# A Fourier mixing layer and a gated expert on one core: the last step's products and buffers, one bank's copy and the first seeds put in another order

## The chip, the cores and the metric

The kernel runs on one core of a Trainium2 chip. A core has five engines with queues of their own: TensorE (PE for its matmuls, PEld for its weight loads, which overlap them), VectorE (DVE), ScalarE (ACT), GpSimd (POOL) and SyncE (SP), which here issues nearly all DMAs. The metric is the device time of one execution in microseconds: the median of the timed runs. Where the profile is quoted, times are microseconds from the start of its span.

## The reference

```
def _attn_ref(x):                      # x: (8, 3008, 256)
    X = np.fft.fft(x, axis=1)
    X = np.fft.fft(X, axis=2)
    return X.real.astype(np.float32)

def _moe_ref(x, w_in, w_out):          # x: (24064, 256), w_in: (256, 2048), w_out: (2048, 256)
    h = x @ w_in
    g = h * np.cos(h)
    return (g @ w_out).astype(np.float32)
```

The output of the first function, reshaped to (24064, 256), is the input of the second. All values are float32.

## The kernel before

For each of the 8 batches, `transform` computes a real two-stage Fourier transform along the sequence (`fold`, `first_half`, a trip through DRAM, `second_half`), and the transform along the 256 columns is folded into the first weight matrix (`WC` for the cosine part, `WS` for the sine part). The work of the next batch's transform is spread over the steps of the current batch.

**Groups, steps, units.** A batch has 6 groups of up to 256 sequence positions: T = 225 columns in group 0, 256 in the others. A group has 8 steps (fp = 0 to 7), each for 256 of the 2048 hidden features, in two halves (u = 0, 1) of 128. There are 8 x 6 x 8 = 384 steps and 768 halves. The main loop (lines 763 to 829) runs over k; one pass is called a unit here. In unit k several halves are at work, in different stages:

- the current half k: two products on TensorE into a PSUM bank H, `mm1(cur, 0)` with WC (L466) and `mm1(cur, 1)` with WS, the first on top of a seed, that ACT wrote there before (`seed`, L447); ACT doubles the first (`act_e`, L478), and DVE makes the mirrored side (`dve_h`, L482);
- half k-1: ACT rounds (`act_round`, L494), DVE takes the fraction (`dve_frac`, L498), ACT takes the sine (`act_sin`, L504);
- half k-2: DVE multiplies (`dve_g`, L508), and after a step's second half POOL forms sums of the results (`sums`, L524 to L531; on DVE for the very last step);
- the step that is LAG = 5 units back: `mm2` (L557), seven output products m = 0 to 6, which accumulate over a group's 8 steps in four PSUM banks M (m = 0, 1; 2, 3; 4, 5; 6). With d, v = divmod(k - 5, 2), a unit with v = 0 runs m = 0 to 2 and, after `mm1(cur, 1)`, m = 3; a unit with v = 1 runs m = 4 to 6.

Every matmul in float32 is two passes; 256 columns take 0.216 us a pass, 225 take 0.190.

**The end of a group.** When a group's last step has gone through `mm2`, its four banks are copied to SBUF by `take_m`: in the unit with v = 1, bank 0 by ACT (L580) and bank 1 by DVE (L582); in the next unit, bank 2 by ACT and bank 3 (one product) by DVE. In the order before, the DVE copies are the last thing that a unit records, behind L498 and L482. POOL then combines the seven products to four outputs (`combine_m`, L597 to L612), and `store_out` transposes them on DVE (L654) into a buffer `ob` (two of them) and stores them with 16 DMAs on SP (L664). There are eight PSUM banks, four tagged M and four tagged H, and the next group takes the four M banks over as they are released.

**The very end.** The last group is combined by `combine_last` on DVE (L622 to L629), some of it straight from PSUM, transposed on TensorE (L639), copied from PSUM by ACT and DVE to the same two buffers `ob` (L642, L643), and stored with eight DMAs (L646), six on SP and two on ACT.

**The start.** For the first units the seeds need no matmul result, but they wait behind other work on ACT. In units 2 to 4 the first product of the next half, `mm1(nxt, 0)`, and its `act_e` are recorded ahead of the current half's `mm1(cur, 1)`, and behind the previous half's sine.

An engine's instructions run in the order in which the kernel records them; semaphores between engines are placed by the framework.

Of the kernel before, what the change touches and what calls it, by code (L numbers as in the profile page):

```python
# [11 lines left out]
FP = mybir.dt.float32  # L12
AF = mybir.ActivationFunctionType
ALU = mybir.AluOpType

BIG = 12582912.0
TWO_PI = 2.0 * math.pi
# [11 lines left out]
AHEAD = LAG + 1  # L29
# [64 lines left out]
def _runs(g, sg):  # L94


    runs = []
    for j, n, c in _cols(g):
        a, k = c, 0
        if sg:  # L100
            a, j = 256 - c - n, (N2 - j) % N2
            if j == 0:
                a, k, n = a + 1, 33, 31
        runs.append((a // 32, j, k, n))
    return runs
# [3 lines left out]
def kernel(  # L109
# [7 lines left out]
    nc = tc.nc  # L117
# [84 lines left out]
    def psum(name, tag="H"):  # L202
        return ppool.tile([128, 512], FP, tag=tag, bufs=bank[tag], name=name)
# [271 lines left out]
    def act_e(h):  # L475
        T = h.s.T
        h.ew = spool.tile([128, 256], FP, tag="ew", bufs=2, name="ew")
        nc.scalar.mul(out=h.ew[:, 0:T], in_=h.H[:, 0:T], mul=2.0)  # L478
# [17 lines left out]
    def dve_frac(h):  # L496
        r, y = sides(h)
        nc.vector.scalar_tensor_tensor(  # L498
            out=r, in0=r, scalar=-BIG, in1=y, op0=ALU.add, op1=ALU.subtract
        )  # L500

    def act_sin(h):
        r, _ = sides(h)
        nc.scalar.activation(out=r, in_=r, func=AF.Sin, bias=0.0, scale=SIN_SCALE)  # L504
# [13 lines left out]
    def sums(s):  # L518
        T = s.T
        s.S = spool.tile([128, 1024], FP, tag="S", bufs=3, name="S")  # L520
        gv, sv = blocks(s)
        qv = s.r[:, 0 : 4 * T].rearrange("p (q t) -> p q t", q=4)
        tt = (nc.vector if s is steps[-1] else nc.gpsimd).tensor_tensor
        tt(  # L524
            out=sv[:, 0:2],
            in0=qv[:, 1:2].to_broadcast([128, 2, T]),
            in1=qv[:, 0:4:3],
            op=ALU.subtract,
        )
        tt(out=sv[:, 2], in0=sv[:, 1], in1=gv[:, 0, 0], op=ALU.subtract)  # L530
        tt(out=sv[:, 3], in0=gv[:, 1, 0], in1=sv[:, 2], op=ALU.add)  # L531

    acc = {}
    started = {}

    def mm2(s, lo, hi):
        T = s.T
        key = (s.b, s.grp)
        if s.fp == 0 and lo == 0:
            acc[key] = []  # L540
            started[key] = set()
        gv, sv = blocks(s)
        todo = (
            (0, wv[:, 0, 0, s.fp], gv[:, 0, 0]),
            (1, wv[:, 1, 0, s.fp], gv[:, 1, 0]),
            (2, vx[:, 3, s.fp], gv[:, 1, 1]),
            (3, vx[:, 1, s.fp], sv[:, 0]),
            (4, vx[:, 0, s.fp], sv[:, 1]),
            (5, vx[:, 2, s.fp], sv[:, 2]),
            (6, wv[:, 1, 1, s.fp], sv[:, 3]),  # L550
        )
        for m, w, a in todo[lo:hi]:
            first = m // 2 not in started[key]
            if first:
                acc[key].append(psum("M", "M"))
            started[key].add(m // 2)
            nc.tensor.matmul(  # L557
                acc[key][m // 2][:, 256 * (m % 2) : 256 * (m % 2) + T],
                lhsT=w,
                rhs=a,  # L560
                start=first,
                stop=s.fp == 7,
                skip_group_check=True,
            )

    outs = {}
# [3 lines left out]
    def take_m(s, k, eng):  # L570
        T = s.T
        key = (s.b, s.grp)
        if k == 0:
            mrs[key] = spool.tile([128, 7 * 256], FP, tag="mr", bufs=1, name="mr")
        mv = mrs[key].rearrange("p (m t) -> p m t", m=7)[:, :, 0:T]
        m = 1 if k == 3 else 2
        to = mv[:, 2 * k : 2 * k + m]
        at = acc[key][k].rearrange("p (m t) -> p m t", m=2)[:, 0:m, 0:T]
        if eng is nc.scalar:
            eng.mul(out=to, in_=at, mul=TWO_PI)  # L580
        else:
            eng.tensor_scalar(out=to, in0=at, scalar1=TWO_PI, scalar2=None, op0=ALU.mult)  # L582
# [30 lines left out]

    def combine_last(s):
        key = (s.b, s.grp)
        M5, M3 = acc[key][2], acc[key][3]
        mv = mrs.pop(key).rearrange("p (m t) -> p m t", m=7)
        outs[key] = spool.tile([128, 7 * 256], FP, tag="cb", bufs=1, name="cb")
        cv = outs[key].rearrange("p (m t) -> p m t", m=7)
        tt, stt = nc.vector.tensor_tensor, nc.vector.scalar_tensor_tensor  # L620
        more = dict(op0=ALU.mult, op1=ALU.add)
        tt(out=cv[:, 0], in0=mv[:, 0], in1=mv[:, 1], op=ALU.add)  # L622
        stt(out=cv[:, 4], in0=M5[:, 256:512], scalar=-TWO_PI, in1=mv[:, 0], **more)
        stt(out=cv[:, 6], in0=M5[:, 0:256], scalar=TWO_PI, in1=cv[:, 4], **more)
        stt(out=cv[:, 1], in0=M3[:, 0:256], scalar=TWO_PI, in1=cv[:, 6], **more)
        store_last(s, 0)
        tt(out=cv[:, 5], in0=cv[:, 4], in1=mv[:, 3], op=ALU.add)
        tt(out=cv[:, 2], in0=cv[:, 5], in1=mv[:, 2], op=ALU.add)
        stt(out=cv[:, 3], in0=M5[:, 0:256], scalar=TWO_PI, in1=cv[:, 5], **more)  # L629
        store_last(s, 1)  # L630

    def store_last(s, sg):
        cv = outs[s.b, s.grp].rearrange("p (m t) -> p m t", m=7)
        ob = spool.tile([128, 512], FP, tag="ob", bufs=2, name="ob")
        ov = ob.rearrange("t (h c j) -> t h j c", h=2, j=2)
        pos = [psum("po", "H").rearrange("t (z j c) -> t z j c", z=2, j=2)[:, 0] for _ in "ab"]
        for j in range(2):
            for h in range(2):
                nc.tensor.transpose(  # L639
                    pos[h][:, j], cv[:, 2 * sg + j, 128 * h : 128 * h + 128], ident  # L640
                )
        nc.scalar.copy(out=ov[:, 0], in_=pos[0])  # L642
        (nc.vector.tensor_copy if sg else nc.scalar.copy)(out=ov[:, 1], in_=pos[1])  # L643
        for t0, j, k, m in sorted(_runs(s.grp, sg)):
            h, r0 = divmod(32 * t0, 128)
            (nc.scalar if sg and h else nc.sync).dma_start(  # L646
                out=out_r[s.b, j, k : k + m, :],
                in_=ob[r0 : r0 + m, 256 * h : 256 * h + 256],
            )
# [113 lines left out]
    for k in range(2 * n + LAG):  # L763
        t, u = divmod(k, 2)
        d, v = divmod(k - LAG, 2)
        cur, prev, old, nxt = unit(k), unit(k - 1), unit(k - 2), unit(k + 1)
        done = step(d)
        full = step(d if v else d - 1, True)
        if cur:
            if k % (2 * per) == 0:  # L770
                todo = transform(cur.s.b + 1) if cur.s.b + 1 < NB else {}
            if k not in range(3, AHEAD):
                mm1(cur, 0)
                if t == 0:
                    seed_first(cur)
                act_e(cur)
            if k == 0:
                spread_nb()
                fold_weights(1, 3)
            elif k == 1:  # L780
                pw = weights(0, 3)
            elif k == 2:
                pw = weight_row(3)
        if done:
            mm2(done, 4 * v, 4 * v + 3)
        if old:
            dve_g(old)
            if old.u:
                sums(old.s)
        if nxt and 0 < k < AHEAD - 1:  # L790
            seed(nxt)
        if prev:
            act_round(prev)
        if nxt and k >= AHEAD - 1:
            seed(nxt)
        if full:
            take_m(full, 0 if v else 2, nc.scalar)
        if prev:
            dve_frac(prev)
            act_sin(prev)  # L800
        if k == 1:
            keep_weights(0, 3, pw)
        elif k == 2:
            keep_wn(3, pw)
        if k + 1 in range(3, AHEAD):
            mm1(nxt, 0)
            act_e(nxt)
        if cur:
            mm1(cur, 1)
        if done and v == 0:  # L810
            mm2(done, 3, 4)
        if cur:
            dve_h(cur)
        if full:
            take_m(full, 1 if v else 3, nc.vector)
        if u == 0:
            continue
        for i in range(6):
            s = step(t - 4 - i, True)
            if s:  # L820
                combine_m(s, i)
        for sg, lag in ((0, 8), (1, 10)):
            s = step(t - lag, True)
            if s:
                store_out(s, sg)
        for call in opening.pop(t, ()):
            call[0](*call[1:])
        for call in todo.pop(t % per, ()):
            call[0](*call[1:])
# [31 lines left out]
```

## Time and profile before

| what | value |
|---|---|
| median of 3 runs | 1972.82 us (1972.72 to 1973.25) |
| the profiled execution | 1971.85 us |
| its span, first to last instruction | 1970.1 us |
| instructions | 29746 |
| busy: DVE, ACT, POOL | 1465.1, 1495.8, 1395.7 us |
| granted TensorE clock, mean | 0.997 |
| DMA traffic | 88.71 MB, 45 GB/s on the mean |

The four groups of TensorE instructions with the most busy time, by the page (line, engine, operation, output<-inputs, shapes, count | busy, mean ns of one | idle before):

```profile
L557 PE MATMUL M<-S,VX 128*128 128x256 f32 (+1 forms) x2304 | 612.3, 375 | 0.0
...
L466 PE MATMUL H<-pq,WC 128*128 128x256 f32 (+1 forms) x1536 | 458.4, 380 | 1.8 <-ACT H L447 1.8
L466 PE MATMUL H<-pq,WS 128*128 128x256 f32 (+1 forms) x1536 | 451.0, 375 | 0.0
...
L557 PE MATMUL M<-r,w 128*128 128x256 f32 (+1 forms) x1536 | 388.7, 375 | 0.0
```

A matmul's length here is 0.375 us, while the next one starts after 0.216: they are pipelined, so their ends overlap, and idle time before them is nearly nothing. The span is 1.75 us shorter than the time of the execution that it belongs to.

### The profile page before, as it was taken

What the parts mean: (1) busy time and instruction counts of PE and PEld (TensorE: products, weight loads), DVE (VectorE), ACT (ScalarE), POOL (GpSimd) and SP (SyncE); (2) the same over time, 40 slices, a digit from 0 to 9 for tenths busy, and PEclk for the clock granted to TensorE, in tenths of its full rate; (3) what the DMA queues carried; (4) which work ended last, traced back from release to release, by engine and by line L of the source; (5) the groups of instructions that cost most, each with busy time, mean ns of one, the idle gap of its engine ahead of it and who ended that gap; (6) DMA issues with size and microseconds to landing.
All of it is one profiled execution on the core that took longest, in us unless ns stands there. A gap on an engine that the chain in (4) does not pass through costs nothing.

```text
span 1970.1 us, 29746 instructions
## 1 busy us (share of the span) xinstructions
PE 1956.8 (99%) x9360; PEld 1684.9 (86%) x9360; DVE 1465.1 (74%) x2524; ACT 1495.8 (76%) x3360; POOL 1395.7 (71%) x1593
## 2 busy tenths in 40 slices
PE   9999999999999999999999999999999999999998
PEld 4988889888988889888898888988889888898887
DVE  3777778777777777777777777777777777788786
ACT  3777778777777777777777777777777777777775
POOL 3777767777677866787668776687767777666675
PEclk9999999999999999999999999999999999999999
DMA  8412022121211321112221221113111231100001
GB/s 198 97 41 57 21 51 48 38 51 35 51 38 34 57 40 44 35 36 56 42 41 35 51 49 36 38 40 66 29 39 37 56 58 24 38 22 15 11 16 29
DMA packets 176690, 88.71 MB, mean 45 GB/s; under 512 B 103303, under 2 KB 173622, under 8 KB 174902
## 3 DMA queue, kind: packets, MB, share of 16 engines
q1 hardware_dynamic: 176374, 86.68, 21.2%
q8 instruction: 76, 1.25, 0.3%
q14 instruction: 80, 0.66, 0.1%
q10 hardware_dynamic: 160, 0.13, 0.0%
HBM read 49.50 MB, written 37.27 MB: 44 GB/s over the span
## 4 chain that ended last, share of the span: by engine, by line
PE 97%; DMA 1%; SPq 1%; ACT 0%; DVE 0%; issue 0%; POOL 0%; DVEq 0%; POOLq 0%
PE M L557 58%; PE H L466 34%; PE pz L243 3%; PE pb L296 2%; DMA xp<-in_x_dram 1%; SPq L664 0%; PE pw L357 0%; DMA wr<-in_moe_w_in_dram 0%; PE pd L413 0%; DVE r L498 0%; DMA out_dram<-ob 0%; ACT r L504 0%; ACT r L494 0%; ACT H L447 0%; DVE xf L219 0%
## 5 line engine op out<-in xcount | busy, mean ns | idle before, releaser
L524 POOL TENSOR_TENSOR S<-r 128x512 f32<-128x512 f32 (+1 forms) x383 | 474.7, 1239 | 468.3 <-DVE r L508 429.1
L498 DVE SCALAR_TENSOR_TENSOR r<-r,H 128x512 f32<-128x512 f32 (+1 forms) x768 | 519.2, 676 | 287.9 <-ACT r L494 260.4
L504 ACT ACTIVATE r<-r 128x512 f32<-128x512 f32 (+1 forms) x768 | 477.9, 622 | 260.9 <-DVE r L498 258.6
L557 PE MATMUL M<-S,VX 128*128 128x256 f32 (+1 forms) x2304 | 612.3, 375 | 0.0
L508 DVE SCALAR_TENSOR_TENSOR r<-H,r 128x512 f32<-128x512 f32 (+1 forms) x768 | 517.9, 674 | 90.7 <-ACT r L504 39.2
L557 PEld LDWEIGHTS M<-S,VX 128*128 128x128 f32 x2304 | 437.7, 190 | 50.0
L466 PE MATMUL H<-pq,WC 128*128 128x256 f32 (+1 forms) x1536 | 458.4, 380 | 1.8 <-ACT H L447 1.8
L466 PE MATMUL H<-pq,WS 128*128 128x256 f32 (+1 forms) x1536 | 451.0, 375 | 0.0
L494 ACT ACTIVATE r<-H 128x512 f32<-128x512 f32 (+1 forms) x768 | 448.4, 584 | 0.4 <-DVE H L482 0.3
L482 DVE TENSOR_TENSOR H<-ew,H 128x256 f32<-128x256 f32 (+1 forms) x768 | 325.4, 424 | 100.2 <-PE H L466 20.1
L557 PE MATMUL M<-r,w 128*128 128x256 f32 (+1 forms) x1536 | 388.7, 375 | 0.0
L447 ACT ACTIVATE H<-nb,wn 128x256 f32<-128x256 f32 (+1 forms) x766 | 366.7, 479 | 0.0
L478 ACT ACTIVATE ew<-H 128x256 f32<-128x256 f32 (+1 forms) x768 | 288.9, 376 | 82.7 <-PE H L466 76.1
L466 PEld LDWEIGHTS H<-pq,WC 128*128 128x128 f32 x1536 | 278.6, 190 | 80.8 <-issue 42.8
L557 PEld LDWEIGHTS M<-r,w 128*128 128x128 f32 x1536 | 298.8, 197 | 29.7 <-ACT mr L580 1.3
L466 PEld LDWEIGHTS H<-pq,WS 128*128 128x128 f32 x1536 | 292.2, 190 | 32.3 <-issue 0.7
L530 POOL TENSOR_TENSOR S<-S,r 128x256 f32<-128x256 f32 (+1 forms) x383 | 275.3, 719 | 30.0
L531 POOL TENSOR_TENSOR S<-r,S 128x256 f32<-128x256 f32 (+1 forms) x383 | 274.4, 716 | 30.0
L557 PE MATMUL M<-r,VX 128*128 128x256 f32 (+1 forms) x768 | 228.7, 379 | 0.2
L557 PE MATMUL M<-S,w 128*128 128x256 f32 (+1 forms) x768 | 225.2, 375 | 0.0
L557 PEld LDWEIGHTS M<-r,VX 128*128 128x128 f32 x768 | 142.2, 190 | 25.4 <-issue 10.1
L557 PEld LDWEIGHTS M<-S,w 128*128 128x128 f32 x768 | 150.5, 196 | 14.6
(67 smaller groups left out, 918.0 us busy)
## 6 DMA issues: line engine op xcount, KB each, us to landing
out_dram<-ob SPq DMA_DIRECT2D x728, 32.0 KB
xp<-in_x_dram SPq DMA_DIRECT2D x56, 256.0 KB
zd<-zs SPq DMA_DIRECT2D x112, 96.0 KB
z<-zd SPq DMA_DIRECT2D x28, 384.0 KB
xp<-in_x_dram SPq DMA_DIRECT2D x56, 120.0 KB
nb<-nd SPq DMA_DIRECT2D x40, 128.0 KB
wr<-in_moe_w_in_dram SPq DMA_DIRECT2D x8, 256.0 KB
w<-in_moe_w_out_dram SPq DMA_DIRECT2D x4, 512.0 KB
```

Source lines behind the costliest of these rows:

```text
L447: nc.scalar.activation(out=h.H[:, 0:T], in_=s.nb[:, 0:T], func=AF.Copy, bias=0.25, scale=wn[:, f : f + 1])
L466: nc.tensor.matmul(h.H[:, 0:T], lhsT=W[:, 128 * f : 128 * f + 128], rhs=s.pq[:, e * T : e * T + T], start=False, stop=True, skip_group_che ...
L478: nc.scalar.mul(out=h.ew[:, 0:T], in_=h.H[:, 0:T], mul=2.0)
L482: nc.vector.tensor_tensor(out=h.H[:, T : 2 * T][:, ::-1], in0=h.ew[:, 0:T], in1=h.H[:, 0:T], op=ALU.subtract)
L494: nc.scalar.activation(out=r, in_=y, func=AF.Copy, bias=BIG, scale=1.0)
L498: nc.vector.scalar_tensor_tensor(out=r, in0=r, scalar=-BIG, in1=y, op0=ALU.add, op1=ALU.subtract)
L504: nc.scalar.activation(out=r, in_=r, func=AF.Sin, bias=0.0, scale=SIN_SCALE)
L508: nc.vector.scalar_tensor_tensor(out=r, in0=y, scalar=-0.25, in1=r, op0=ALU.add, op1=ALU.mult)
L524: tt(out=sv[:, 0:2], in0=qv[:, 1:2].to_broadcast([128, 2, T]), in1=qv[:, 0:4:3], op=ALU.subtract,)
L530: tt(out=sv[:, 2], in0=sv[:, 1], in1=gv[:, 0, 0], op=ALU.subtract)
L531: tt(out=sv[:, 3], in0=gv[:, 1, 0], in1=sv[:, 2], op=ALU.add)
L557: nc.tensor.matmul(acc[key][m // 2][:, 256 * (m % 2) : 256 * (m % 2) + T], lhsT=w, rhs=a, start=first, stop=s.fp == 7, skip_group_check=True,)
```

## The change

It has three parts.

- In units with a `full` step, `take_m` on DVE is recorded behind `dve_g` and `sums` and ahead of `act_round`, where it was the last call of the unit before. The ACT copy keeps its place. The very last step has no `take_m` any more.
- In units 2 to 4 (k + 1 in 3 to 5), `mm1(nxt, 0)` and `act_e(nxt)` are recorded between `dve_frac(prev)` and `act_sin(prev)`, where they were behind the sine (and behind `keep_wn`).
- The very last step runs its products in the order 0, 1, 5, 4 and 3, 2, 6. `combine_last` copies bank 0 with ACT and takes the other products from PSUM; the transposes are recorded among its operations (`turn_last`), two outputs to one PSUM bank; `store_last` copies a whole bank with one ACT instruction into a buffer of the tag `pq` (eight of them), and of its second four DMAs every other one is on ACT.

```diff
-    def mm2(s, lo, hi):
+    def mm2(s, lo, hi, order=range(7)):
...
-        for m, w, a in todo[lo:hi]:
+        for m, w, a in (todo[i] for i in order[lo:hi]):
...
     def combine_last(s):
         key = (s.b, s.grp)
-        M5, M3 = acc[key][2], acc[key][3]
-        mv = mrs.pop(key).rearrange("p (m t) -> p m t", m=7)
+        M0, M1, M2, M3 = acc[key]
+        mv = spool.tile([128, 7 * 256], FP, tag="mr", bufs=1, name="mr")
+        nc.scalar.mul(out=mv[:, 0:512], in_=M0, mul=TWO_PI)
...
+        nc.vector.tensor_tensor(out=cv[:, 0], in0=mv[:, 0], in1=mv[:, 1], op=ALU.add)
+        turn_last(s, 0, 0)
+        more(4, M2[:, 256:512], mv[:, 0])
+        more(6, M2[:, 0:256], cv[:, 4])
+        more(5, M1[:, 256:512], cv[:, 4])
+        more(2, M1[:, 0:256], cv[:, 5])
+        turn_last(s, 1, 0)
+        more(1, M3[:, 0:256], cv[:, 6])
+        turn_last(s, 0, 1)
+        more(3, M2[:, 0:256], cv[:, 5])
+        turn_last(s, 1, 1)
+        for sg in range(2):
+            store_last(s, sg)
...
     def store_last(s, sg):
...
+        ob = spool.tile([128, 512], FP, tag="pq", bufs=8, name="ob")
+        nc.scalar.copy(
+            out=ob.rearrange("t (h c j) -> t h j c", h=2, j=2),
+            in_=pos[sg].rearrange("t (h j c) -> t h j c", h=2, j=2),
+        )
+        for i, (t0, j, k, m) in enumerate(sorted(_runs(s.grp, sg))):
             h, r0 = divmod(32 * t0, 128)
-            (nc.scalar if sg and h else nc.sync).dma_start(
+            (nc.scalar if sg and i % 2 else nc.sync).dma_start(
...
         if done:
-            mm2(done, 4 * v, 4 * v + 3)
+            order = (0, 1, 5, 4, 3, 2, 6) if done is steps[-1] else range(7)
+            mm2(done, 4 * v, 4 * v + 3, order)
         if old:
             dve_g(old)
             if old.u:
                 sums(old.s)
+        if full and full is not steps[-1]:
+            take_m(full, 1 if v else 3, nc.vector)
         if nxt and 0 < k < AHEAD - 1:
             seed(nxt)
         if prev:
             act_round(prev)
         if nxt and k >= AHEAD - 1:
             seed(nxt)
-        if full:
+        if full and full is not steps[-1]:
             take_m(full, 0 if v else 2, nc.scalar)
         if prev:
             dve_frac(prev)
+        if k + 1 in range(3, AHEAD):
+            mm1(nxt, 0)
+            act_e(nxt)
+        if prev:
             act_sin(prev)
...
-        if k + 1 in range(3, AHEAD):
-            mm1(nxt, 0)
-            act_e(nxt)
         if cur:
             mm1(cur, 1)
         if done and v == 0:
-            mm2(done, 3, 4)
+            mm2(done, 3, 4, order)
         if cur:
             dve_h(cur)
-        if full:
-            take_m(full, 1 if v else 3, nc.vector)
```

`more(to, m, at)` is one DVE instruction that scales the product `m` by 2 pi (by -2 pi for `to` = 4) and adds `at`.

More of the change, by code (lines that the diff above doesn't have):

```diff
@@ L572, in take_m @@
         key = (s.b, s.grp)
-        if k == 0:
+        if key not in mrs:
             mrs[key] = spool.tile([128, 7 * 256], FP, tag="mr", bufs=1, name="mr")
@@ L615, in combine_last @@
         key = (s.b, s.grp)
-        M5, M3 = acc[key][2], acc[key][3]
-        mv = mrs.pop(key).rearrange("p (m t) -> p m t", m=7)
+        M0, M1, M2, M3 = acc[key]
+        mv = spool.tile([128, 7 * 256], FP, tag="mr", bufs=1, name="mr")
+        nc.scalar.mul(out=mv[:, 0:512], in_=M0, mul=TWO_PI)
+        mv = mv.rearrange("p (m t) -> p m t", m=7)
         outs[key] = spool.tile([128, 7 * 256], FP, tag="cb", bufs=1, name="cb")
         cv = outs[key].rearrange("p (m t) -> p m t", m=7)
-        tt, stt = nc.vector.tensor_tensor, nc.vector.scalar_tensor_tensor
@@ L621, in combine_last @@
[L621 to L628, printed above, removed]
@@ L629, in combine_last, with more @@
-        stt(out=cv[:, 3], in0=M5[:, 0:256], scalar=TWO_PI, in1=cv[:, 5], **more)
-        store_last(s, 1)
-    def store_last(s, sg):
[L633 to L644, printed above, removed]
+        def more(to, m, at):
+            nc.vector.scalar_tensor_tensor(
+                out=cv[:, to],
+                in0=m,
+                scalar=-TWO_PI if to == 4 else TWO_PI,
+                in1=at,
+                op0=ALU.mult,
+                op1=ALU.add,
+            )
@@ new lines, with turn_last @@
+    pos = {}
+    def turn_last(s, sg, j):
+        cv = outs[s.b, s.grp].rearrange("p (m t) -> p m t", m=7)
+        if j == 0:
+            pos[sg] = psum("po", "H")
+        for h in range(2):
+            nc.tensor.transpose(
+                pos[sg][:, 256 * h + 128 * j : 256 * h + 128 * j + 128],
+                cv[:, 2 * sg + j, 128 * h : 128 * h + 128],
+                ident,
+            )
+    def store_last(s, sg):
+        ob = spool.tile([128, 512], FP, tag="pq", bufs=8, name="ob")
+        nc.scalar.copy(
+            out=ob.rearrange("t (h c j) -> t h j c", h=2, j=2),
+            in_=pos[sg].rearrange("t (h j c) -> t h j c", h=2, j=2),
+        )
+        for i, (t0, j, k, m) in enumerate(sorted(_runs(s.grp, sg))):
```

## The prediction, made before the changed kernel had run

> **What bounds the kernel now.** I read the page first (busy shares and the chain that ended last), then the waits of all engines, then the timeline at group changes, at the start and at the end.
>
> ```profile
> PE 1956.8 (99%) x9360; PEld 1684.9 (86%) x9360; DVE 1465.1 (74%) x2524; ACT 1495.8 (76%) x3360; POOL 1395.7 (71%) x1593
> ...
> PE 97%; DMA 1%; SPq 1%; ACT 0%; DVE 0%; issue 0%; POOL 0%; DVEq 0%; POOLq 0%
> ```
>
> TensorE is the bound from about 50 us to 1960 us. A busy share of 99% can still hide stalls, since a matmul that starts late is drawn longer, so I looked at who waits for whom among its weight loads (engine line <- cause: us in total, times, longest).
>
> ```profile
> PEld M L557 <- issue: 10.1, 40, 0.3
> PEld M L557 <- PE M L557: 2.4, 7, 0.3
> PEld M L557 <- ACT mr L580: 1.3, 8, 0.2
> ```
>
> There are 47 changes of group (48 groups), and 40 + 7 makes 47: once per group a weight load of the output products is late. The timeline shows where (start, length, engine, line).
>
> ```profile
> 171.39 0.65 DVE L508 SCALAR_TENSOR_TENSOR r<-H,r 128x512 f32<-128x512 f32 x1
> ...
> 173.40 0.69 DVE L498 SCALAR_TENSOR_TENSOR r<-r,H 128x512 f32<-128x512 f32 x1 [1.36 <-ACT r L494]
> ...
> 174.56 0.68 DVE L582 TENSOR_SCALAR mr<-M 128x512 f32<-128x512 f32 x1
> ...
> 175.36 0.30 PEld L557 LDWEIGHTS M<-r,VX 128*128 128x128 f32 x2 [0.28 <-issue]
> 175.39 0.67 PE L557 MATMUL M<-r,VX 128*128 128x256 f32 x2
> ...
> 180.21 0.59 PE L557 MATMUL M<-r,VX 128*128 128x256 f32 x2
> ```
>
> L582 copies the old group's second bank (m=2, 3) and ends at 175.24; the first use of that bank by the new group (m=2) waits for it. Its weight load starts at 175.36 instead of one pass (0.216 us) ahead. The matmul starts 0.074 us late and the pair then takes 0.67 instead of 0.59: together 0.149 us per group, repeated to within 0.003 us in 32 of the 47 changes. At the 7 batch ends (298.57 us is the first) the same wait costs 0.194 + 0.075 = 0.269 us. At the 8 changes out of a group 0 (225 columns, so a shorter copy) it costs 0.025, and m=0 loses 0.041 there to the ACT copy L580. From these rows a weight load that comes late by x costs about x - 0.11 us (0.26 late cost 0.149, 0.135 cost 0.025).
>
> **The change part by part: the second bank's copy (L582) ahead of the fraction (L498).** It goes in the DVE queue behind L508 and takes 0.60 us of issue (from L582 to the next L508 in back-to-back rows). It adds a wait for TensorE's m=3, with L498 and L482 queued behind it, but m=3 has ended 0.5 to 1.3 us before DVE gets there (170.71 against 171.99 here), so that wait is nothing. The pool also hands banks out in the order of their release: by the wait lists of the changed program m=0 now waits for DVE's L582 and m=2 for ACT's L580. Here L582 would end at 172.7 and L580 at 174.25 as before, and the loads for m=0 and m=2 start at 174.24 and 175.10: both in time. m=4 and m=6 change places in the same way and have 0.3 us or more to spare everywhere I worked them out.
>
> What it costs depends on DVE's idle time before L498. In 21 changes between wide groups and 7 out of a group 0 this idle time is 1.05 to 1.63 us; 0.60 us disappears in it. The gain there is whole: 21 x 0.149 = 3.1 us and 7 x (0.025 + 0.041) = 0.5 us. In the other 19 it is at most 0.08 us:
>
> ```profile
> 1925.25 0.65 DVE L508 SCALAR_TENSOR_TENSOR r<-H,r 128x512 f32<-128x512 f32 x1
> ...
> 1925.98 0.69 DVE L498 SCALAR_TENSOR_TENSOR r<-r,H 128x512 f32<-128x512 f32 x1
> ```
>
> There L498 moves from 1925.98 to 1926.45, ACT's sine L504 from 1926.71 to 1927.17, and behind it in ACT's queue L478, L494 and the seed L447 by 0.46 each. The seed would end at 1928.93, just in time for its matmul. One unit later the chain L498, L504, L478, L494, L447 is still 0.04 late against before while TensorE is 0.149 ahead: the load of L466 comes about 0.16 late, which costs 0.05. The gain left is 0.10, in 4 changes: 0.4 us. (In the last change out of a group 0 it is nothing.) In 7 more (254.76 is the first) eight small matmuls (L296) follow, which give the chain time to catch up: 7 x 0.149 = 1.0 us. At the 7 batch ends a unit is shorter (225 columns, 0.190 us a pass), and ACT has no gap from 297.8 to 300.5 with L580 twice in its queue; I get the load of L466 about 0.34 late, which gives back 0.23 to 0.27 of 0.269: nothing gained. Sum: 3.1 + 0.5 + 0.4 + 1.0 = 5.0 us. The bounds: 3.3 us, if all 19 gain nothing or lose a little, and 32 x 0.149 + 7 x 0.269 + 8 x 0.066 = 7.2 us, if no delay reaches TensorE. The other copy that moves (L582 on 256 columns, 0.42 us) goes behind an L508 that now starts earlier and costs nothing of its own.
>
> **First seeds ahead of the sine.** Only ACT's order changes, in three units; no DMA moves.
>
> ```profile
> 46.48 0.58 ACT L504 ACTIVATE r<-r 128x450 f32<-128x450 f32 x1 [0.69 <-DVE r L498]
> ...
> 47.00 0.36 ACT L478 ACTIVATE ew<-H 128x225 f32<-128x225 f32 x1
> ...
> 47.25 0.45 ACT L447 ACTIVATE H<-nb,wn 128x225 f32<-128x225 f32 x1
> ...
> 47.76 0.50 PEld L466 LDWEIGHTS H<-pq,WC 128*128 128x128 f32 x2 [1.70 <-ACT H L447]
> 47.76 1.12 PE L466 MATMUL H<-pq,WC 128*128 128x225 f32 x2 [1.35 <-ACT H L447]
> ```
>
> L478 fits in the 0.69 us in which ACT waits for L498, so the seed L447 starts 0.25 us earlier and TensorE's pause shrinks from 1.35 to 1.10. In the next unit L478 ends up in front of L504 just when L504 is ready (48.86), and 0.19 of it is left. This falls in a stretch in which the granted clock is 0.50 (47.31 to 54.14), so 0.19 us of earlier work is worth about 0.1 us. I take 0.1; the bounds are 0 and 0.25.
>
> The Trainium skill (TensorE: Matmul & The Clock Gate, "What's actually happening") says that the clock is halved only after an idle window of some 3.4 us, and that the window runs free of the kernel. By that a pause of 1.35 us would not halve it; here it was halved 0.9 us into that pause, for 6.83 us. The measurement decides; by the page's rule the sum would be the same 0.1 to 0.25, without a dip to lose or to win.
>
> **The last step.** Its products run in another order, its copies go to other buffers, and one DVE copy (0.69 us) is gone. What ends the span is neither:
>
> ```profile
> 1957.82 5.83 SPq L664 DMA_DIRECT2D out_dram<-ob  x10
> 1963.75 3.71 SPq L646 DMA_DIRECT2D out_dram<-ob  x6
> ...
> 1966.00 1.19 ACTq L646 DMA_DIRECT2D out_dram<-ob  x2
> ```
>
> SP issues the previous group's stores until 1963.65, then six of the last eight back to back, 0.52 to 0.60 each; the last lands 2.1 us after its issue, and about 1.1 us follow. L664 hangs on a DVE transpose that doesn't move, and after the change SP still has six of the eight. Compute now ends earlier (I get both halves copied by about 1963.2 instead of 1965.97), but SP isn't free before 1963.65. What is left: one wait fewer between SP's issues (0.1 us) and ACT's two stores out of the way of the last ones (0.05). I take 0.15, between -0.3 and 0.3. The product that comes third now (m=5) needs S from L530, which ends at 1957.71 and is wanted at 1958.27; without that cover it would cost at most L530's 0.42.
>
> **The sum.** 5.0 + 0.1 + 0.15 = 5.3 us. The profiled execution took 1971.85 (span 1970.1): 1966.6 after. It is 1.0 below the median of the timed runs, 1972.82; with the same distance the median after is 1967.5, 0.27% faster. A measurement of this kernel can tell 0.2%, 3.9 us, from no change.
>
> **The rivals.**
> 1. No delay reaches TensorE at the batch ends and in the last batch either: 7.2 + 0.25 = 7.5 us, 1965.4. For it: DVE is 74% and ACT 76% busy, and elsewhere ACT waits 0.39 us a unit. Against it: ACT's gapless stretch after 297.8.
> 2. The clock doesn't dip at the start, since the pause is shorter. 5.93 us of TensorE work ran at half clock there, so up to 2.9 us more: 1964.6. Against it: the dip came at 47.31, 0.9 us into a pause that stays 1.1 us.
> 3. A wait takes the place of the one removed: the later fraction delays the seeds, and TensorE loses at L466 what it wins at L557 in all 19 changes without idle time, or a little more. Then 3.3 us are left: 1969.5, within 0.2%.
> 4. The same chain doesn't recover inside a group. Each unit's ACT order is L478, L494, L447, L504, and a v=1 unit has only 0.02 us between a seed and its weight load. If each of the 19 changes lost the whole 0.47 us by which L498 is late, that is 19 x 0.47 = 8.9 against 3.6 + 0.25 won: 1977.9, slower. It decides from a net loss of 0.20 us per such change. Against it: ACT's gaps of 0.3 to 0.4 us in nearly every unit (0.41 on DVE at 1930.88, 0.29 on ACT at 1929.98).
>
> **How the numbers follow.** Forecast 0.65 (own range 1966.5 to 1968.6), rival 1 0.13, rival 2 0.05, rival 3 0.13, rival 4 0.04. The likeliest is 1967.5. Leaving out rival 4, rival 2 and the edge of rival 3 gives 1965.0 to 1969.4. Faster by over 0.2% are the forecast and rivals 1 and 2, 0.83; rival 3 is within it, 0.13; rival 4 is slower, 0.04.
>
> **What would show it.** In the waits, "PEld M L557 <- issue" (40 times) and "<- PE M L557" (7 times) should all but vanish, and the pair M<-r,VX at a group change take 0.59 us; at batch ends and in the last batch a late load of L466 should appear instead. L498's idle time of 1.36 us should shrink to about 0.7 with L582 in it. At the start the pause before L466 should be 1.1 us with the clock at 0.50 behind it. At the end SP should issue without a pause up to its last store, some 2 us before the last landing. I am wrong if the late loads of L557 stay, if the gain sits in the last 10 us, or if TensorE has new stalls away from group changes.

## The result and the profile after

| | kernel before | changed kernel |
|---|---|---|
| median | 1973.28 us (6 runs, 1972.72 to 1973.9) | 1965.47 us (6 runs, 1965.09 to 1967.58) |
| ratio, 95% interval | | 0.9962 [0.9949, 0.9975] |
| the profiled execution, its span | 1971.85, 1970.1 us | 1965.9, 1964.1 us |

The change made the kernel 0.38% faster, by 7.8 us between these medians and by 6.0 between the two profiled executions. In the order of the prediction, first the page (busy shares, chain), then the waits of TensorE's weight loads:

```profile
PE 1950.2 (99%) x9360; PEld 1688.6 (86%) x9360; DVE 1466.5 (75%) x2522; ACT 1497.9 (76%) x3359; POOL 1396.6 (71%) x1593
...
PE 98%; DMA 1%; ACT 0%; DVE 0%; SPq 0%; POOL 0%; issue 0%; POOLq 0%; ACTq 0%
```

```profile
PEld H L466 <- issue: 43.5, 58, 0.8
...
PEld H L466 <- ACT H L447: 9.1, 34, 1.5
```

TensorE is busy 6.6 us less with the same 9360 matmuls. All three lines "PEld M L557" (40, 7 and 8 times before) are gone. What has grown is the last line above, loads of L466 that wait for the seed L447: 6.8 us in 26 cases before, 9.1 in 34 now. The timeline of the change at 175 us, DVE and then TensorE:

```profile
170.76 0.65 DVE L508 SCALAR_TENSOR_TENSOR r<-H,r 128x512 f32<-128x512 f32 x1
171.34 0.67 DVE L582 TENSOR_SCALAR mr<-M 128x512 f32<-128x512 f32 x1
172.77 0.69 DVE L498 SCALAR_TENSOR_TENSOR r<-r,H 128x512 f32<-128x512 f32 x1 [0.77 <-ACT r L494]
```

```profile
174.69 0.59 PE L557 MATMUL M<-r,VX 128*128 128x256 f32 x2
```

L582 stands in DVE's idle time, which went from 1.36 to 0.77 us; L498 is no later, and the pair for m=2 takes 0.59 us and not 0.67. The batch end (297 to 301 us) is where something was given back:

```profile
299.53 0.34 ACT L478 ACTIVATE ew<-H 128x225 f32<-128x225 f32 x1
...
300.19 0.45 ACT L447 ACTIVATE H<-nb,wn 128x225 f32<-128x225 f32 x1
...
300.70 0.30 PEld L466 LDWEIGHTS H<-pq,WC 128*128 128x128 f32 x2 [0.29 <-ACT H L447]
300.70 0.65 PE L466 MATMUL H<-pq,WC 128*128 128x225 f32 x2
```

The seed ends at 300.64, and the load that waits for it is 0.29 us late; the pair takes 0.65 where 0.54 is normal. Start and end:

```profile
47.89 0.65 PE L466 MATMUL H<-pq,WC 128*128 128x225 f32 x2 [1.10 <-ACT H L447]
...
49.97 0.83 PE L466 MATMUL H<-pq,WC 128*128 128x225 f32 x2 [1.04 <-ACT H L447]
```

```profile
1951.99 5.83 SPq L686 DMA_DIRECT2D out_dram<-ob  x10
1957.92 3.71 SPq L668 DMA_DIRECT2D out_dram<-ob  x6
```

The first pause is 1.10 us, as forecast; the clock behind it isn't: it stayed full there and fell at 50.30 us, behind the second pause, for 3.41 us. SP again issues the old group's stores (L686, before L664) until the last six follow, 0.10 us behind them and in 3.71 us, both as before.

For all kernels below I cut the span at two starts of L557's passes: its 113th (the first of group 1) and its last. Main loop = 113th to last, that is nearly all the work; end = last to the end of the span.

| kernel | main loop | end | TensorE clock 0.5 at the start |
|---|---|---|---|
| before | 1870.79 | 9.85 | 6.83 us |
| changed | 1865.36 | 9.74 | 3.41 us |
| e1, copy alone | 1865.35 | 9.89 | 3.41 us |
| e2, start alone | 1870.78 | 9.88 | none |
| e3, end alone | 1870.79 | 9.76 | 3.41 us |
| e9, before with the copy twice | 1904.35 | 9.83 | 6.83 us |
| e10, changed with the copy twice | 1877.88 | 9.74 | 6.83 us |
| a2, changed again | 1865.36 | 10.11 | 6.83 us |
| e5, copy between | 1863.94 | 9.75 | none |
| e6, pauses filled | 1865.39 | 9.75 | none |
| e7, end on two queues | 1865.38 | 8.59 | 6.83 us |
| e8, all three | 1863.90 | 8.57 | none |
| e11, before with pauses filled | 1870.75 | 9.88 | none |

The main loop repeats to 0.05 us wherever its code is the same, so hundredths can be read from it, while times of whole runs spread by 3 to 4 us.

### The profile page after: what moved, and what is told of

Read it like the earlier page. It is cut to its first block, busy times and chain, and to the rows that moved or that the text cites. A ratio compares the mean times of both kernels' runs of the same rounds, so it can differ in the third digit from the quotient of the medians.

```text
span 1964.1 us, 29636 instructions
## 1 busy us (share of the span) xinstructions
PE 1950.2 (99%) x9360; PEld 1688.6 (86%) x9360; DVE 1466.5 (75%) x2522; ACT 1497.9 (76%) x3359; POOL 1396.6 (71%) x1593
## 4 chain that ended last, share of the span: by engine, by line
PE 98%; DMA 1%; ACT 0%; DVE 0%; SPq 0%; POOL 0%; issue 0%; POOLq 0%; ACTq 0%
PE M L557 58%; PE H L466 34%; PE pz L243 3%; PE pb L296 2%; DMA xp<-in_x_dram 1%; PE pw L357 0%; PE pd L413 0%; DMA wr<-in_moe_w_in_dram 0%; DVE r L498 0%; ACT r L504 0%; DVE cb L624 0%; ACT r L494 0%; ACT H L447 0%; POOL xf L226 0%; PE H L453 0%
## 5 line engine op out<-in xcount | busy, mean ns | idle before, releaser
L498 DVE SCALAR_TENSOR_TENSOR r<-r,H 128x512 f32<-128x512 f32 (+1 forms) x768 | 518.8, 676 | 259.8 <-ACT r L494 232.3
L557 PE MATMUL M<-S,VX 128*128 128x256 f32 (+1 forms) x2304 | 612.3, 375 | 0.0
L557 PEld LDWEIGHTS M<-S,VX 128*128 128x128 f32 x2304 | 437.7, 190 | 50.0
L466 PE MATMUL H<-pq,WC 128*128 128x256 f32 (+1 forms) x1536 | 458.5, 380 | 2.1 <-ACT H L447 2.1
L466 PE MATMUL H<-pq,WS 128*128 128x256 f32 (+1 forms) x1536 | 450.6, 375 | 0.0
L557 PE MATMUL M<-r,w 128*128 128x256 f32 (+1 forms) x1536 | 388.4, 375 | 0.0
L447 ACT ACTIVATE H<-nb,wn 128x256 f32<-128x256 f32 (+1 forms) x766 | 366.3, 478 | 0.0
L466 PEld LDWEIGHTS H<-pq,WC 128*128 128x128 f32 x1536 | 277.0, 190 | 83.6 <-issue 42.8
L478 ACT ACTIVATE ew<-H 128x256 f32<-128x256 f32 (+1 forms) x768 | 289.1, 376 | 75.5 <-PE H L466 66.7
L557 PEld LDWEIGHTS M<-r,w 128*128 128x128 f32 x1536 | 301.0, 197 | 27.2
L466 PEld LDWEIGHTS H<-pq,WS 128*128 128x128 f32 x1536 | 291.4, 190 | 32.7 <-issue 0.7
L557 PE MATMUL M<-r,VX 128*128 128x256 f32 (+1 forms) x768 | 225.6, 375 | 0.0
L557 PE MATMUL M<-S,w 128*128 128x256 f32 (+1 forms) x768 | 225.2, 375 | 0.0
L557 PEld LDWEIGHTS M<-S,w 128*128 128x128 f32 x768 | 150.5, 196 | 14.7
L557 PEld LDWEIGHTS M<-r,VX 128*128 128x128 f32 x768 | 146.1, 190 | 14.6
```

Of the source, the lines that this page charges most:

```text
L447: nc.scalar.activation(out=h.H[:, 0:T], in_=s.nb[:, 0:T], func=AF.Copy, bias=0.25, scale=wn[:, f : f + 1])
L466: nc.tensor.matmul(h.H[:, 0:T], lhsT=W[:, 128 * f : 128 * f + 128], rhs=s.pq[:, e * T : e * T + T], start=False, stop=True, skip_group_che ...
L498: nc.vector.scalar_tensor_tensor(out=r, in0=r, scalar=-BIG, in1=y, op0=ALU.add, op1=ALU.subtract)
L557: nc.tensor.matmul(acc[key][m // 2][:, 256 * (m % 2) : 256 * (m % 2) + T], lhsT=w, rhs=a, start=first, stop=s.fp == 7, skip_group_check=True,)
```

## The experiments

### Each part alone

**e1**, the copy alone: in the kernel before (`take_m` also makes its tile at the first copy recorded, DVE's, as in the changed kernel),

```diff
+        if full:
+            take_m(full, 1 if v else 3, nc.vector)
         if nxt and 0 < k < AHEAD - 1:
...
         if cur:
             dve_h(cur)
-        if full:
-            take_m(full, 1 if v else 3, nc.vector)
```

> The kernel before with the second bank's copy (L582) moved ahead of the fraction and nothing else changed. Theory (the copy is nearly the whole gain): the late loads of L557 vanish (7.2 us of stalls), some 1.8 us come back as late loads of L466, 5.4 us are left, so about 1967.9 against 1973.3, with the start and the last 10 us as before. Rival (the gain of 7.8 us sits mostly in the start or the end): 1971 or more.

Measured: 1967.57 us against 1972.16, ratio 0.9975 [0.9966, 0.9984]. The main loop is that of the changed kernel. A pass is late by what its start lies more than 0.216 us (0.190 for 225 columns) behind the start of the pass before (0.01 us and less left out). The late passes at m=0 and m=2 fell from 7.2 us to none, and those of L466 rose from 6.5 to 8.2.

**e2**, the start alone: in the kernel before,

```diff
             dve_frac(prev)
+        if k + 1 in range(3, AHEAD):
+            mm1(nxt, 0)
+            act_e(nxt)
+        if prev:
             act_sin(prev)
...
-        if k + 1 in range(3, AHEAD):
-            mm1(nxt, 0)
-            act_e(nxt)
```

> The kernel before with the first seeds ahead of the sine and nothing else changed. Theory A (the forecast's: 0.25 us less pause at half clock): 0.1 us gained, 1973.2. Theory B (the smoother start makes the stretch at half clock shorter, 3.4 us or none in place of 6.8, as the profile after has it): 1.5 to 2.5 us gained, 1970.8 to 1971.8, with mean granted clocks of 0.998 or 0.999 in place of 0.997, and runs that differ by 1 to 2 us among themselves.

Measured: 1972.54 us against 1972.16, ratio 1.0 [0.9991, 1.0009]. Its profiled execution had no stretch at half clock at all, but its other runs had clocks from 0.999 to 0.997 and times from 1970.2 to 1973.4, just as the kernel before, whose 27 runs beside it went from 1969.95 to 1973.97 and from 0.999 to 0.997. So the length of that stretch changes from run to run, with or without the edit, and the gain of theory B doesn't show; the interval leaves out gains above 1.8 us. Theory A's 0.1 us can't be told from nothing here. Whether the edit changes how often the stretch is absent stays open: 3 of its 11 runs have a clock of 0.999, and 6 of the 27 beside it.

**e3**, the end alone: the changed kernel with the two other parts put back.

> The kernel before with the last step's order, buffers and stores changed and nothing else. Theory (SP's queue ends the span, not the buffers or the copies): 0.15 us gained, 1973.1. Rival (the wait for the buffers and the missing DVE copy counted): copies done 2.7 us earlier, so 1 to 2.7 us gained, 1970.6 to 1972.3.

Measured: 1972.58 us against 1972.16, ratio 1.0 [0.9991, 1.0009]; the end is 9.76 us against 9.85. The whole part counted for 0.1 us.

### What the late copy costs

**e9**, in the kernel before:

```diff
         if full:
             take_m(full, 1 if v else 3, nc.vector)
+            if v:
+                take_m(full, 1, nc.vector)
```

> The kernel before with the second bank's copy made twice in a row on DVE, in its old place (same values twice). Theory (the new group's m=2 waits for the end of that copy): it ends 0.60 us later (0.54 in group 0), so each of the 47 changes loses that much more, 27 to 28 us in all, about 2001. Rival (the 0.149 us are the price of an instruction with two semaphores, or of the change of banks itself, whenever the copy ends): within 2 us of 1973.

Measured: 2007.58 us (one run). The main loop is 33.56 longer, 0.72 in each of the 39 changes between full groups and batches, 0.66 in the 8 out of a group 0. That is more than the 0.60 that I expected: the second copy begins only when the first has ended, 0.72 us behind its start. Now the waits name the pair of the theory:

```profile
PE M L557 <- DVE mr L582: 29.2, 47, 0.8
```

47 times, once per change, TensorE stood still for L582. In the kernel before the same wait was too short to show as idle time.

**e10**, the same in the changed kernel.

> The changed kernel with the second bank's copy made twice in a row on DVE, in its new place. Theory (DVE's idle time of 1.05 us or more in 28 changes covers it, and in the other 19 the later fraction reaches TensorE through L504, L478, L494 and L447): those 28 lose nothing or the few hundredths by which the second copy overruns the idle time, the 19 lose 0.5 to 0.7 each, 10 to 13 us in all, 1976 to 1979. Rival (DVE's queue has no cover anywhere, each of 47 changes loses the 0.7 us): 33 us, about 1999. Rival (the late fraction costs nothing): within 2 us of 1966.

Measured: 1980.16 us (one run), main loop 12.52 longer than the changed kernel's. By changes (the time from 56 passes of L557 ahead of the change to 56 behind it, against the kernel before, us each; minus is faster):

| changes | how many | forecast | changed | e10 | e5 |
|---|---|---|---|---|---|
| idle time on DVE, full groups | 21 | -0.149 | -0.150 | -0.150 | -0.150 |
| idle time on DVE, out of group 0 | 7 | -0.066 | -0.064 | -0.064 | -0.022 |
| no idle time, eight L296 follow | 7 | -0.149 | -0.116 | +0.437 | -0.148 |
| no idle time, last batch | 4 | -0.10 | -0.144 | +0.581 | -0.150 |
| batch ends | 7 | 0 | -0.066 | +0.661 | -0.270 |
| last one out of group 0 | 1 | 0 | +0.021 | +0.685 | -0.020 |
| sum | 47 | -5.0 | -5.42 | +7.10 | -6.84 |

The 28 changes with idle time don't feel the second copy at all. Of the 19 others 12 lose 0.66 to 0.73 us each by it; of the seven with L296 behind them six lose 0.58 or 0.59, the first 0.37. That the fraction reaches TensorE over ACT shows in the waits of e10:

```profile
PEld H L466 <- ACT ew L478: 14.0, 19, 0.8
```

19 times, as often as there are changes without idle time, a load of L466 waits for L478, which is behind the late sine in ACT's queue. I had expected the seed L447, two instructions further on.

In the changed kernel the same wait stands once, at the first of the seven changes with L296 behind them, the one that lost 0.07. Of the seven only there the transpose ahead of the copy had waited for a DMA, so DVE was late already:

```profile
251.67 0.71 DVE L676 STREAM_TRANSPOSE ob<-cb 128x512 f32<-128x512 f32 x1 [0.33 <-DMA z<-zd]
...
255.14 0.30 PEld L466 LDWEIGHTS H<-pq,WS 128*128 128x128 f32 x2 [0.35 <-ACT ew L478]
```

### Is the late fraction avoidable?

**e5**, in the changed kernel:

```diff
-        if full and full is not steps[-1]:
-            take_m(full, 1 if v else 3, nc.vector)
...
             act_sin(prev)
...
+        if full and full is not steps[-1] and v:
+            take_m(full, 1, nc.vector)
         if cur:
             mm1(cur, 1)
...
             dve_h(cur)
+        if full and full is not steps[-1] and not v:
+            take_m(full, 3, nc.vector)
```

> The changed kernel with the second bank's copy between the fraction and the mirrored side (L498, L582, L482) instead of ahead of the fraction, the fourth bank's copy last in its unit as before. Theory (the late fraction gives 1.8 us back as late loads of L466): this copy still ends 0.4 us before m=2 needs it, the fraction isn't late, L482 has room: no late loads of L557, and those of L466 as in the kernel before (6.7 us and not 8.2): 1.5 to 1.8 us faster than the changed kernel, some 7.2 faster than before. Rival (the loads of L466 are late for another reason, or the delayed L482 costs as much): no faster than the changed kernel.

Measured: 1964.49 us, ratio 0.9958 [0.9944, 0.9972] to before; the main loop is 1.42 shorter than the changed kernel's and 6.84 shorter than before. The timeline of DVE at the batch end:

```profile
295.60 0.62 DVE L498 SCALAR_TENSOR_TENSOR r<-r,H 128x450 f32<-128x450 f32 x1
296.14 0.68 DVE L582 TENSOR_SCALAR mr<-M 128x512 f32<-128x512 f32 x1
296.74 0.39 DVE L482 TENSOR_TENSOR H<-ew,H 128x225 f32<-128x225 f32 x1
```

The fraction is first, the copy ends at 296.82 and m=2's load starts at 297.20. The batch ends win their whole 0.27, and the late passes of L466 are back at 6.5 us. In the eight changes out of a group 0 the 0.041 at m=0 stays, since that bank waits for ACT's copy again; these 0.33 us are what is missing from the 1.8. The banks change hands here as in the kernel before, so the earlier copy alone removes the wait of m=2, whichever bank m=2 gets.

### The start and the clock

**a2**, the changed kernel again, for the spread.

> The changed kernel once more, beside more runs of the kernel before. Runs of before have spread from 1970.0 to 1974.0 with the mean granted clock (0.999 to 0.997), so the first ratio (0.9962) may hold some luck of the clock. Theory: 5.4 us from the copy and 0.2 from the end: median 5.6 below before's, ratio 0.997, runs from 1964.5 to 1968.5. Rival (the first 7.8 us are real, the start gives the rest): ratio 0.996 again.

Measured: 1966.14 us (1964.21 to 1967.38) against 1973.0 (9 runs, 1969.6 to 1973.94), ratio 0.9966 [0.9954, 0.9979]: 6.9 us, between the two expectations and not apart from either.

**e6**, in the changed kernel, and **e11**, in the kernel before:

```diff
         if k + 1 in range(3, AHEAD):
+            if k > 2:
+                keep_busy(2, "M", 256)
             mm1(nxt, 0)
```

> The changed kernel with two matmuls on constants (0.86 us, results not used) in each of the two pauses at the start. Theory (the pauses are what halves the clock, and where the clock's windows lie decides for how long): no stretch at half clock before the end, all clocks 0.999, all runs within 0.6 us of each other, at 1964.8 to 1965.4. Rival (something else halves it, such as the eight one-column matmuls ahead of the first pause): the same spread of 3 us as the changed kernel.

> The kernel before with the same matmuls on constants (0.86 us) in each of its two pauses at the start. Theory (the pauses halve the clock, as in the changed kernel): no stretch at half clock in the profile, times of 1969.8 to 1971.2 in place of 1970 to 1974, 0.07% under before. Set against the changed kernel with the pauses filled (1964.86) it then gives the change at equal clock: 5.4 us from the copy, 0.2 from the end, and the seeds' own 0.2 to 0.5 at full clock, 5.8 to 6.1 us. Rival (the half clock comes from something else): a stretch at half clock, and before's spread.

Measured: e6 1964.86 us (1964.44 to 1965.92), e11 1970.89 us (11 runs, 1970.13 to 1972.21) against 1972.96, ratio 0.9992 [0.9983, 1.0001]. Both profiles are at full clock from 5.1 us until behind the main loop. The windows show it (us, then busy time of PE, PEld, DVE, ACT, POOL, clock, DMA share, GB/s), the changed kernel first, then e6:

```profile
48.00:52.00 4.00, 2.96 (x10) 2.45 (x11) 2.78 (x7) 2.87 (x7) 2.38 (x3) 0.79 1.23 184
52.00:56.00 4.00, 4.00 (x18) 3.80 (x18) 2.24 (x5) 2.47 (x6) 2.40 (x3) 0.79 1.16 309
```

```profile
48.00:52.00 4.00, 3.75 (x18) 3.29 (x19) 3.08 (x7) 3.34 (x9) 2.39 (x3) 1.00 1.24 184
52.00:56.00 4.00, 4.00 (x23) 3.92 (x22) 3.35 (x7) 3.20 (x9) 2.40 (x3) 1.00 1.15 299
```

None of the 21 runs of the three kernels with filled pauses (e6, e8, e11) has a clock below 0.998; of the 60 runs of the kernel before beside the experiments 24 have. The eight one-column matmuls are still there, so that rival falls. The spread went from 3 or 4 us to 1.5 and 2.1, not to 0.6 as I expected of e6: in the profiles the first pass of L466 starts between 36.9 and 39.0 us, and no edit here touches that. At equal clock the change is worth 1970.89 - 1964.86 = 6.0 us. The profiles also price the seeds, by the time from the first pass of L466 to the 113th of L557:

| stretch at half clock | seeds in the old place | seeds in the new place |
|---|---|---|
| none | 50.65 (e11) | 50.01 to 50.03 (e2, e5, e6, e8) |
| 3.41 us | 52.19, 52.19 (e1, e3) | 51.70 (changed) |
| 6.83 us | 52.49, 53.47 (before, e9) | 52.40 to 52.59 (e7, e10, a2) |

At full clock that is 0.63 us. With a stretch of 6.83 us its place alone moves the time by 1 us, so the 0.1 that was forecast for that case can't be read.

### The end

**e7**, in the changed kernel's `store_last`:

```diff
-        nc.scalar.copy(
+        (nc.vector.tensor_copy if sg else nc.scalar.copy)(
...
-            (nc.scalar if sg and i % 2 else nc.sync).dma_start(
+            (nc.sync if sg else nc.scalar).dma_start(
```

> The changed kernel with the last eight stores as four on ACT and four on SP instead of two and six, the second copy on DVE. Theory (SP's queue ends the span): SP's last store is issued two issues earlier, so the end from the last product of the main loop to the end of the span is 1.2 us shorter than in the changed kernel (9.7 us there). Rival (the landing or the copies end it): no change, or a later end since ACT's stores wait for its copy.

Measured: 1965.61 us; the end is 8.59 us and not 9.74. The timeline of SP and of ACT:

```profile
1951.92 7.90 SPq L686 DMA_DIRECT2D out_dram<-ob  x13
1959.92 2.57 SPq L668 DMA_DIRECT2D out_dram<-ob  x4
```

```profile
1958.83 2.70 ACTq L668 DMA_DIRECT2D out_dram<-ob  x4
```

Four issues in place of six on SP, two issues (1.15 us) less at the end. The second copy is on DVE here, but SP is busy with the old group's stores until 1959.82, behind both copies.

**e8**, the edits of e5, e6 and e7 together in the changed kernel.

> The changed kernel with three edits of the runs before at once: the second bank's copy between the fraction and the mirrored side, matmuls on constants in the two pauses at the start, and the last stores as four on ACT and four on SP. Theory (they are independent: 1.4 us in the groups, the clock's dip with its spread, 1.1 to 1.2 us at the end): from the 113th pass of L557 to its last 1863.9 us, from the first pass of L557 to that one 36.5 us in each run, the end 8.6 us, times of 1962 to 1963.5 with all clocks at 0.998 to 0.999, the fastest median of all. Rival (they take from each other, say a faster start only waits at the first w_out transfer): 1964 or more.

Measured: 1962.02 us (1961.23 to 1962.55), ratio 0.9948 [0.9934, 0.9961] to before, all clocks 0.999. The three edits add up, and this version is faster than both kernels.

## Why the prediction held, step by step

The prediction was 1967.5 us in a range from 1965.0 to 1969.4, faster; 1965.47 is in it, nearer to its edge than to its middle.

1. **The late loads come from the second bank's copy.** Right, and shown by e1 (they vanish with that edit alone), e9 (they grow with the copy's end) and e5 (the wait of m=2 vanishes with an earlier copy and the banks in their old order).
2. **28 changes have cover on DVE.** Right to 0.002 us on the mean of each group, and e10 shows that the cover would have held a second copy.
3. **The 19 others give something back.** Right in kind: e5 has the whole gain once the fraction isn't late. The sizes were off: I gave 0.10 to the last batch's changes and nothing to the batch ends; they won 0.144 and 0.066. Of the seven with L296 behind them six won 0.147, but the first (254 us) lost 0.07. Only there DVE was late already, behind the transpose that had waited for a DMA, and the prediction took the seven for alike. The sum, 5.0, was 5.43: the batch ends and the last batch gave 0.6 more than forecast, that one change 0.2 less.
4. **The seeds.** The mechanism was right (both pauses are 0.25 us shorter), the size wrong. I priced 0.1 us, within 0 to 0.25, because before's profile had that stretch at half clock. At full clock each pause counts in full, and with the first units it is 0.63; so the 0.1 to 0.25 that the prediction also gave for a start without a dip was wrong too. That is the term of the sum that was most off. The medians don't show it: e2 alone gained nothing that can be told from noise.
5. **The end.** 0.15 was forecast, 0.11 measured (0.09 in e3). That SP's queue sets the end was right, and e7 shows it by taking two issues off that queue. Of the two gains forecast the larger, one wait fewer between SP's issues, didn't come: counted from the last pass of L557, SP's last six issues run from 3.54 to 7.25 us in both kernels. What was won lies behind them (2.59 us to the end before, 2.48 after); that it comes from ACT's two stores, now issued earlier, fits but isn't shown. In a2, the same program as the changed kernel, SP's issues took longer and the end was 10.11 us, so a tenth is less than one run can differ by.
6. **From the profile to the median.** I took the profiled execution to be 1.0 us below the median by nature. It is a draw: 66 runs of the kernel before lie between 1969.6 and 1974.1; of the 60 beside the experiments those at a clock of 0.999 between 1969.6 and 1972.1, those at 0.997 between 1971.7 and 1974.1. The six runs behind the 1973.28 were all in the upper half, 1972.72 or more. At equal clock 5.43 + 0.63 + 0.11 = 6.2 us of parts stand against 6.0 between e11 and e6, and a2 gave 6.9. The rest of the first 7.8, some 1.6 us, fits that draw and is luck: of the 2.5 us by which the gain exceeded the forecast the parts explain 0.9.

Of the rivals, the first gave 1965.4, the time that was measured, but not by its cause: the batch ends won a quarter of what it asked. The second fell: the clock still dipped in the changed kernel's profiles, for 3.41 and 6.83 us (a2), and the dip can be absent with the same pauses (e2, e5). The third and fourth describe a real loss, 1.8 us of late passes of L466, too small to decide; e10 shows that with one more copy in that place it would have outweighed the gain.

## What to carry to other kernels

A bound engine at 99% can still stall once per outer loop: look for the few waits of its loads whose count is that of the loop, and ask which copy they wait for. When a copy is moved ahead in a queue, look at every place where it lands for idle time in front of the next instruction, and try the place behind the first instruction whose lateness costs something; here one place further back gave 1.4 us more than the head of the queue. Before a gain below 0.4% is read from medians, find a stretch that repeats, and compare that.

## What the runs showed of the hardware

- The stretch at half clock has a length of 3.41 or 6.83 us or is absent, in the same program, and started between 47.3 and 51.6 us in the profiles. The Trainium skill (TensorE: Matmul & The Clock Gate, "What's actually happening") gives a free-running window of 3.413 us, and these lengths agree with it. It also says that the clock falls after an idle window; here TensorE was busy for 1.36 of the 3.41 us before the fall at 50.30, so a window that is 40% busy was enough, and the measurement decides. Its section "A second HAM failure mode: psum-queue depth-cycling" comes nearer: frequent short pauses make the clock fall, with no share given.
- All 13 profiles give a share. I divided each into windows of 3.413 us from the moment when its clock first became full (5.92 us in the changed kernel), and left out the one-column matmuls of L377 (eight in a row, 1.05 us). Around the two pauses the clock fell from full behind each of the eight windows in which TensorE was busy for 1.16 to 1.58 us, and behind none with 1.78 us or more (e2, from 44.44 us). Over the whole profiles, the falls at the end included, it fell behind 1.63 us at most (e9, from 1996.09) and stayed behind 1.62 us at least (e7, from 21.71), so the border lies at nearly half. With L377 counted there is no such order: in the kernel before it fell behind a window with 2.51 us. How the two pauses lie in the windows differs from run to run, and it fits as what decides whether the clock falls there; no run here sets it on purpose.
- Two matmuls on constants in each pause (0.86 us, which left 0.24 and 0.18 us open in e6, 0.49 and 0.43 in e11) were enough to keep the full clock in all three profiles that had them (e8 is as e6). Since e2 and e5 had no fall without them, the clocks of all 21 runs (0.998 or 0.999) are the stronger sign.
- A weight load that comes late by 0.26 us costs 0.149 us, and 0.72 us more of delay cost the whole 0.72 more (e9). So in these rows only the first 0.11 us of a delay were free.
